# Attention and routed adapters on one core: PSUM planned by the bank, and new rules and priorities for the order of loads and work

## Chip, cores and metric

The kernel runs on one core of a Trainium2 chip. The metric is the device time of one execution in microseconds (us). Before the change three timed runs gave 164.81, 165.91 and 168.38 us; the median is 165.91.

## The reference

Inputs q, k and v have the shape (8 batches, 8 heads, 576 positions, 64). First comes attention in a sliding window, then a mixture of small adapters on its output:

```python
def _attn_ref(q, k, v):
    scores = scale * np.matmul(q, k.transpose(0, 1, 3, 2))      # scale = 1/sqrt(64)
    mask = np.abs(pos[:, None] - pos[None, :]) <= 32
    attn = softmax(np.where(mask, scores, -1e9))
    return np.matmul(attn, v)

def _moe_ref(x, w_gate, A, B):                                  # x: (4608, 512)
    logits = x @ w_gate                                         # 8 experts
    # the two largest logits of each row, softmax over the two: w
    # delta = sum over the two experts e of w_e * (x @ A[e]) @ B[e],  rank 16
    return x + delta
```

## The kernel before, in words

**Attention.** q and k arrive in nine tiles of 128 rows. A row is 16 consecutive positions of a head, for two heads (`raw`, three buffers for q and three for k). The loads are issued by GpSimd (`load`, L272, issue at L279) and turn float32 into float16 on the way. TensorE transposes a tile with 64 matmuls (`trans`, L360). VectorE copies q's transposes to `qT` (L367), ScalarE copies k's to `kT` (L372). A score task (`score`, L404 for the mask and L416 for the products) fills one 128x1024 float32 piece of PSUM, and ScalarE turns it into `PT` by an exp (L424). There are 36 score tasks. v comes in float32 by four loads per batch from the SP queue (`load_v`, L289) into two `vraw` buffers; GpSimd casts each half of a batch into one of three `vbd` buffers (`cast_v`, L339). A pv task (L465) multiplies PT by v for one pair of heads; there are four in a batch, 32 in all. VectorE divides by the row sums (`norm`, L483 and L484) and writes float16 rows `xs`.

**Adapters.** For each batch TensorE transposes `xs` (L518), VectorE copies the result to `xT` (L523), and TensorE makes the products with A and the gate weights (`moe_zl`, L531). ScalarE copies these to `zl` (L542), except for the last batch. The choice of two experts is a chain: two VectorE operations (L554, L555), an exp on ScalarE (L558), six on VectorE (L562 to L568), and two multiplications (`gate3`, L574 and L575), which run on GpSimd, on VectorE for the last batch. TensorE transposes the result `zs` (L581), ScalarE copies it to `zT` (L586), and TensorE makes delta plus x in pairs of matmuls (L594 and L596). ScalarE copies the sums to `ob` (L603) and SP stores them (L609, L614).

**What sets the order.** No order is written by hand. `Planner` (L24) runs once on the host when the kernel is built. Each piece of work is a task with an engine, an assumed duration, a due time, dependencies, and slots that it takes from and gives back to named pools. The planner steps through its own clock and starts, on each engine, the ready task with the lowest due time whose slots are free; DMA transfers are tasks on two modelled queues, Q0 for GpSimd's loads and Q1 for SP's. The start times that come out fix the order in which the instructions of each engine are issued (L654 to L660), and which buffer each task gets. On the chip each engine works in that order and waits on semaphores; the planner's times play no part there.

PSUM is four tiles `W0` to `W3` of 128x1024 float32, two banks each (L204). Every task that writes PSUM takes a whole `W`. A k load of tile t is made to follow, in the plan and so on GpSimd's queue, the first v cast of batch t-2, by `GATE` (L183), which is empty for tile 1. The adapter weights' loads follow the first load of the second v batch (`WDEP`, L185). Tile 0 is loaded and transposed in two halves (`SPLIT`).

Of the kernel before, what the change touches and what calls it, by code (L numbers as in the profile page):

```python
# [23 lines left out]
class Planner:  # L24
# [4 lines left out]
    STICK = 0.3  # L29
    SWITCH = 0.12  # L30
# [8 lines left out]

    def add(self, name, eng, dur, due, emit, deps=(), take=(), drop=(), lat=None, pkt=1.0,  # L40
            cap=1.0, mode=None):
        t = dict(name=name, eng=eng, dur=dur, due=due, emit=emit, deps=list(deps),
                 take=list(take), drop=list(drop), lat=self.LAT if lat is None else lat,
                 n=len(self.tasks), pkt=pkt, cap=cap, mode=mode)
        assert name not in self.by_name, name
        self.tasks.append(t)
        self.by_name[name] = t
        return name

    def run(self):  # L50
# [9 lines left out]
        held = {}  # L60
# [26 lines left out]
        while events:  # L87
# [17 lines left out]
            while drops and drops[0][0] <= now + 1e-9:  # L105
                _, _, (p, key) = heapq.heappop(drops)
                self.slots[p].append(held.pop((p, key)))
            for e in engines:
                if free_at[e] > now + 1e-9:
                    continue  # L110
                last_mode = mode.get(e)
                for t in sorted(ready[e], key=lambda t: (
                        t["due"] + (self.STICK if t["mode"] != last_mode else 0.0), t["n"])):
                    if all(self.slots[p] for p, _ in t["take"]):
                        break
                else:
                    continue
                ready[e].remove(t)
                for p, key in t["take"]:
                    s = self.slots[p].pop(0)  # L120
                    held[p, key] = s
                t["start"] = now
                end = now + t["dur"] + (self.SWITCH if t["mode"] != last_mode else 0.0)
                mode[e] = t["mode"]
                free_at[e] = end
                heapq.heappush(events, end)
                t["held"] = dict(held)
                done.append(t)
                finish(t, end)
# [16 lines left out]
def kernel(  # L146
# [36 lines left out]
    GATE = {t: [f"cv{t - 2}.0"] for t in range(2, 9)}  # L183
    GATE[1] = []
    WDEP = ["lv1.0.0"]  # L185
# [19 lines left out]
    W16 = [w.bitcast(F16) for w in W]  # L205

# [10 lines left out]
    P.pool("W", NW)  # L217
# [8 lines left out]
    P.pool("rc", 3)  # L226
    place = {}

    def slot(p, key):
        return place[p, key]  # L230

# [89 lines left out]
    for b in range(B):  # L321
        for n, (m0, m1) in enumerate(vparts(b)):
            for h in range(2):
# [3 lines left out]
                      prev, take=[] if n or h else [("vr", b)], lat=1.2)  # L327
                prev = [f"lv{b}.{n}.{h}"]
                P.add(f"dv{b}.{n}.{h}", VQ[h][2], 2.15 * (m1 - m0) / 36, 0, None, prev, lat=0.8,
                      pkt=14.7, cap=0.82)  # L330
    P.add("ldw", "SP", 2.0, -2, load_w, WDEP, lat=1.2)
    P.add("dw", "Q1", 1.7, -10, None, ["ldw"], lat=0.8, pkt=18.0)
# [20 lines left out]
    def trans(t, w, h0, h1):  # L353
        src = raw[2 * slot("raw" + "qk"[w], t) + w]
        tp = W16[slot("W", ("t", t, w, h0))].rearrange("p (h r i) -> p h r i", h=2, i=64)
        for r in range(RR):
            for h in range(h0, h1):
                p = slice(64 * h, 64 * h + 64)
                for hh in range(2):
                    nc.tensor.matmul(out=tp[64 * hh:64 * hh + 64, h, r],  # L360
# [3 lines left out]
    def evac(t, w, h0, h1):  # L364
        tp = W16[slot("W", ("t", t, w, h0))].rearrange("p (h r i) -> p h r i", h=2, i=64)[:, h0:h1]
        if w == 0:
            nc.vector.tensor_copy(  # L367
                out=qT[:, :, PADQ + 128 * t + 64 * h0:PADQ + 128 * t + 64 * h1].rearrange(
                    "p r (h i) -> p h r i", i=64),
                in_=tp)  # L370
        else:
            nc.scalar.copy(  # L372
                out=kT[slot("kT", t)][:, 64 * h0:64 * h1].rearrange("p (h i) r -> p h i r", i=64),
                in_=tp.rearrange("p h r i -> p h i r"))

    for t in range(NTI):
        hs = ((0, 1), (1, 2)) if t in SPLIT else ((0, 2),)
        for w in range(2):
            for y, (h0, h1) in enumerate(hs):
# [7 lines left out]
                      take=[("W", ("t", t, w, h0))] + ([("kT", t)] if w and y == 0 else []),  # L387
                      drop=[("raw" + "qk"[w], t)] if last else [])
                P.add(f"e{'qk'[w]}{t}.{y}", "ACT" if w else "DVE",
                      (0.2 + 1.5 * f) if w else (0.12 + 1.1 * f), due,  # L390
                      lambda t=t, w=w, h0=h0, h1=h1: evac(t, w, h0, h1),
                      [f"tr{t}.{w}.{y}"], drop=[("W", ("t", t, w, h0))])
# [6 lines left out]
    def score(t):  # L399
        ps = W[slot("W", ("s", t))].rearrange("p (e i c) -> p e i c", e=2, c=128)  # L400
# [22 lines left out]
    def expo(t):  # L423
        nc.scalar.activation(out=PTs[slot("PT", t)].rearrange("p e i c -> p (e i c)"),  # L424
                             in_=W[slot("W", ("s", t))],
# [12 lines left out]
    for t in range(NT):  # L438
        need = set()
        for g in blocks(t):  # L440
            lo, hi = 4 * g - 2, 4 * g + 5
            for z in (max(lo, 0), min(hi, NI - 1)):
                tt = z // 128
                need.add((tt, (z % 128) // 64 if tt in SPLIT else 0))
# [8 lines left out]
    def pv(u):  # L453
        b, n = divmod(u, NP)
        e, m = divmod(n, 2)
        po = W[slot("W", ("p", u))].rearrange("p (h c) -> p h c", h=2)
# [21 lines left out]
    def norm(u):  # L478
        b, n = divmod(u, NP)
        po = W[slot("W", ("p", u))].rearrange("p (h c) -> p h c", h=2)[:, :, 0:NG * VD]  # L480
# [29 lines left out]
    GX = ((0, 1, 2, 3), (4,))  # L510

    def moe_xT(b, j):
        x = xs[slot("xs", b)]
        tp = W16[slot("W", ("x", b, j))]
        for m, g in enumerate(GX[j]):
# [5 lines left out]
    def moe_ex(b, j):  # L521
        n = len(GX[j])
        nc.vector.tensor_copy(  # L523
            out=xT[b % 2][:, GX[j][0]:GX[j][0] + n].rearrange("p g c k -> p (g c k)"),
            in_=W16[slot("W", ("x", b, j))][:, 0:512 * n])

    def moe_zl(b):
        pz = W[slot("W", ("z", b))]
# [11 lines left out]
    def copy_z(b):  # L540
        pz = W[slot("W", ("z", b))][:, 0:GS * NG].rearrange("p (g c) -> p g c", c=GS)
        nc.scalar.copy(out=zls[b % 2], in_=pz[:, :, 0:ER + E])  # L542

    def zlog(b):
        if b in DIRECT:
            pz = W[slot("W", ("z", b))][:, 0:GS * NG].rearrange("p (g c) -> p g c", c=GS)
# [23 lines left out]
    def gate3(b):  # L570
        z = zlog(b)[0]
        lm, m2, s, gate = (gt[x][b % 2] for x in ("lm", "m2", "s", "gate"))
        eng = nc.vector if b in DIRECT else nc.gpsimd
# [3 lines left out]
    def moe_zT(b):  # L577
        zs = zss[b % 2].rearrange("p g e r -> p g (e r)")
        tp = W16[slot("W", ("y", b))]
# [4 lines left out]
    def moe_ez(b):  # L584
        tp = W16[slot("W", ("y", b))][:, 0:128 * NG]
# [3 lines left out]

    def moe_pd(b, j):  # L590
        pd = W[slot("W", ("d", b, j))].rearrange("p (i c) -> p i c", c=DD)
# [8 lines left out]
    def moe_eo(b, j):  # L600
        n = len(GG[j])
        pd = W[slot("W", ("d", b, j))].rearrange("p (i c) -> p i c", c=DD)
# [13 lines left out]
    for b in range(B):  # L616
        d0 = 4 * b + 4.6
        for j in range(2):
            n = len(GX[j])
            P.add(f"xT{b}.{j}", "PE", 0.24 * n, d0 + 0.1 * j, lambda b=b, j=j: moe_xT(b, j),  # L620
                  [f"nm{u}" for u in range(4 * b, 4 * b + 4)]
                  + ([f"zl{b - 2}"] if b >= 2 else []), take=[("W", ("x", b, j))], mode="full")
            P.add(f"exx{b}.{j}", "DVE", 0.1 + 0.28 * n, d0 + 0.1 * j - 0.5, lambda b=b, j=j: moe_ex(b, j),
                  [f"xT{b}.{j}"], drop=[("W", ("x", b, j))])
        P.add(f"zl{b}", "PE", 1.29, d0 + 0.5, lambda b=b: moe_zl(b),
              [f"exx{b}.{j}" for j in range(2)] + ["cw"], take=[("W", ("z", b))], mode="full")
        dr = b in DIRECT
        if not dr:
            P.add(f"cz{b}", "ACT", 0.85, d0 - 1, lambda b=b: copy_z(b), [f"zl{b}"]
# [4 lines left out]
        P.add(f"g2{b}", "DVE", 1.15, d0 - 1, lambda b=b: gate2(b), [f"ge{b}"])  # L634
        P.add(f"g3{b}", "DVE" if dr else "POOL", 1.05 if dr else 1.6, d0 - 1,
              lambda b=b: gate3(b), [f"g2{b}"], drop=[("W", ("z", b))] if dr else [])
        P.add(f"zT{b}", "PE", 0.32, d0 + 0.8, lambda b=b: moe_zT(b), [f"g3{b}"],
              take=[("W", ("y", b))], mode="full")
        P.add(f"ez{b}", "ACT", 0.7, d0 + 0.5, lambda b=b: moe_ez(b),
              [f"zT{b}"] + ([f"pd{b - 2}.2"] if b >= 2 else []), drop=[("W", ("y", b))])  # L640
        for j in range(3):
            n = len(GG[j])
            P.add(f"pd{b}.{j}", "PE", 0.44 * n, d0 + 1.2 + 0.7 * j, lambda b=b, j=j: moe_pd(b, j),
                  [f"ez{b}", "perm"] + ([f"pd{b}.{j - 1}"] if j else []),
                  take=[("W", ("d", b, j)), ("ob", (b, j))], drop=[("xs", b)] if j == 2 else [], mode="full")
            P.add(f"eo{b}.{j}", "ACT", 0.2 + 0.42 * n, d0 + 1.2 + 0.7 * j,
                  lambda b=b, j=j: moe_eo(b, j), [f"pd{b}.{j}"],
                  drop=[("W", ("d", b, j))])
            P.add(f"st{b}.{j}", "SP", 0.65 * n, d0, lambda b=b, j=j: moe_st(b, j),
# [44 lines left out]
```

## Time and profile before

| | |
|---|---|
| median of three timed runs | 165.91 us |
| device time of the profiled execution | 168.72 us |
| its span, first to last instruction | 167.0 us |
| mean granted TensorE clock | 0.877 |
| TensorE matmul busy | 104.2 us (62%), 3464 matmuls |
| ScalarE busy | 83.6 us (50%) |
| VectorE busy | 67.8 us (41%) |
| GpSimd busy | 54.0 us (32%) |
| DMA queue of SP (v, weights, stores) | 43824 packets, 19.42 MB, 44.2% of 16 engines |
| DMA queue of GpSimd (q, k) | 5152 packets, 9.44 MB, 33.3% |
| instruction queue q8 | 27 packets, 0.44 MB |

Engine names in the profile: PE is TensorE (PEld its weight loads), DVE VectorE, ACT ScalarE, POOL GpSimd, SP SyncE. A group of instructions is given by line, engine, operation, output and inputs, with the idle time just before it and what ended it ("<-"). "issue" is time in which an engine waited for nothing that the profile shows. In the slices, each digit is the busy share of a fortieth of the span in tenths, PEclk the granted TensorE clock in the same way.

### The profile page before, as it was taken

The numbers are of one execution on the slowest core, as the hardware profiler recorded it, in microseconds if no ns is written. First come the engines' busy times: TensorE is split into PE (matmuls) and PEld (weight loads), VectorE is DVE, ScalarE is ACT, GpSimd is POOL, SyncE is SP. The second block draws the span as 40 slices with busy tenths as digits, with TensorE's granted clock in tenths as the row PEclk, the third lists the DMA queues.
The fourth block names the chain that finished last, engine by engine and source line by source line (L and its number), as shares of the span: only waits on it lengthen the run. The fifth ranks groups of instructions, "written<-read, shape, count | busy, mean of one in ns | idle before, by whom it ended". The sixth has DMA issues, their size and how long they took to land.

```text
span 167.0 us, 7557 instructions
## 1 busy us (share of the span) xinstructions
PE 104.2 (62%) x3464; PEld 77.2 (46%) x3464; DVE 67.8 (41%) x164; ACT 83.6 (50%) x94; POOL 54.0 (32%) x76
## 2 busy tenths in 40 slices
PE   0259536480975857736478678775667989386350
PEld 0247425470864634326457554544457467274110
DVE  0011520270745625225265834763460958542300
ACT  3214706432044497584036479744669796416160
POOL 7950710745030779800000683900063030210000
PEclk9999955558589999996789999999999999959785
DMA  5999999999979669999996279999630254404434
GB/s 86 215 222 224 189 215 226 212 203 206 214 180 205 116 122 183 215 253 221 342 231 164 50 103 253 296 183 216 225 98 4 92 205 145 142 4 147 138 112 171
DMA packets 49008, 29.34 MB, mean 176 GB/s; under 512 B 39632, under 2 KB 39632, under 8 KB 48976
## 3 DMA queue, kind: packets, MB, share of 16 engines
q1 hardware_dynamic: 43824, 19.42, 44.2%
q0 software_dynamic: 5152, 9.44, 33.3%
q8 instruction: 27, 0.44, 1.1%
q14 instruction: 5, 0.04, 0.1%
HBM read 28.85 MB, written 9.44 MB: 229 GB/s over the span
## 4 chain that ended last, share of the span: by engine, by line
PE 39%; issue 30%; DMA 12%; DVE 6%; ACT 4%; POOL 4%; POOLq 1%; ACTq 1%; SPq 0%; DVEq 0%
PE W L518 6%; PE W L465 5%; PE W L360 5%; DMA vraw<-in_v_dram 5%; PE W L594 5%; DMA raw<-in_q_dram 5%; PE W L416 5%; PE W L596 4%; PE W L531 4%; PE W L404 4%; POOL vbd L339 2%; DMA out_dram<-ob 2%; DVE xs L484 2%; ACT PT L424 2%; DVE qT L367 1%
## 5 line engine op out<-in xcount | busy, mean ns | idle before, releaser
L424 ACT ACTIVATE PT<-W 128x1024 f16<-128x1024 f32 x36 | 35.6, 1031 | 29.1 <-PE W L416 25.0
L360 PE MATMUL W<-ident,raw 64*64 64x64 f16 x1152 | 18.6, 210 | 21.4 <-issue 10.9
L465 PE MATMUL W<-vbd,PT 64*64 64x65 f16 x1152 | 19.0, 205 | 16.0 <-issue 11.5
L339 POOL TENSOR_SCALAR_AFFINE_SELECT vbd<-vraw 128x1152 f16<-128x1152 f32 x16 | 20.3, 1274 | 25.6 <-DMA vraw<-in_v_dram 25.5
L603 ACT COPY ob<-W 128x1024 f32<-128x1024 f32 (+1 forms) x24 | 20.6, 872 | 15.7 <-PE W L596 13.0
L360 PEld LDWEIGHTS <-raw 64*64 64x64 f16 x1152 | 16.3, 123 | 22.9 <-issue 12.8
L484 DVE TENSOR_TENSOR xs<-W,rc 128x640 f16<-128x640 f32 x32 | 26.4, 825 | 1.1
L372 ACT COPY kT<-W 128x2048 f16<-128x2048 f16 (+1 forms) x10 | 17.0, 1698 | 18.7 <-PE W L360 18.7
L465 PEld LDWEIGHTS <-PT 64*64 64x64 f16 x1152 | 15.4, 118 | 21.0 <-issue 17.2
L483 DVE RECIPROCAL rc<-W 128x10 f32<-128x10 f32 x32 | 6.9, 217 | 42.2 <-PE W L465 41.3
L416 PE MATMUL W<-qT,kT 64*64 64x128 f16 x576 | 20.4, 246 | 4.3 <-issue 2.8
L574 POOL TENSOR_TENSOR gate<-lm,s 128x40 f32<-128x40 f32 x7 | 1.8, 253 | 65.0 <-DVE s L568 65.0
L416 PEld LDWEIGHTS <-kT 64*64 64x64 f16 x576 | 17.0, 124 | 10.1 <-issue 7.3
L367 DVE COPY qT<-W 128x2048 f16<-128x2048 f16 (+1 forms) x10 | 11.2, 1116 | 24.0 <-PE W L360 24.0
L518 PE MATMUL W<-ident,xs 128*128 128x128 f16 x160 | 14.2, 253 | 6.5 <-issue 5.5
L404 PE MATMUL W<-mask,ident 64*64 64x512 f16 x144 | 17.9, 458 | 0.0
L523 DVE COPY xT<-W 128x2048 f16<-128x2048 f16 (+1 forms) x16 | 12.5, 816 | 10.9 <-PE W L518 10.9
L594 PE MATMUL W<-Bsb,zT 128*128 128x512 f16 x40 | 16.4, 409 | 0.8 <-ACT zT L586 0.8
L518 PEld LDWEIGHTS <-xs 128*128 128x128 f16 x160 | 12.3, 126 | 8.4 <-issue 6.0
L596 PE MATMUL W<-xs,po__107 128*128 128x512 f16 x40 | 16.0, 401 | 0.0
L531 PE MATMUL W<-WA,xT 128*128 128x136 f16 x160 | 11.4, 226 | 1.7 <-issue 1.2
L531 PEld LDWEIGHTS <-xT 128*128 128x128 f16 x160 | 10.0, 99 | 3.0 <-issue 1.3
(40 smaller groups left out, 82.3 us busy)
## 6 DMA issues: line engine op xcount, KB each, us to landing
vraw<-in_v_dram SPq DMA_DIRECT2D x32, 288.0 KB, 7.3
out_dram<-ob SPq DMA_DIRECT2D x8, 512.0 KB, 9.9
out_dram<-ob SPq DMA_DIRECT2D x16, 192.0 KB, 3.6
out_dram<-ob SPq DMA_DIRECT2D x8, 256.0 KB, 2.9
raw<-in_k_dram POOLq DMA_DIRECT2D x4, 256.0 KB, 6.8
raw<-in_q_dram POOLq DMA_DIRECT2D x4, 256.0 KB, 6.1
raw<-in_k_dram POOLq DMA_DIRECT2D x2, 448.0 KB, 6.5
raw<-in_q_dram POOLq DMA_DIRECT2D x2, 448.0 KB, 7.7
```

The lines of the kernel that those rows point to most:

```text
L339: nc.gpsimd.affine_select(out=o, in_=i_, compare_op=ALU.is_ge, fill=0.0, base=1, channel_multiplier=0, pattern=[[0, m1 - m0], [0, D]])
L360: nc.tensor.matmul(out=tp[64 * hh:64 * hh + 64, h, r], lhsT=src[p, hh, D * r:D * r + D], rhs=ident[p, p], is_transpose=True, start=True, s ...
L404: nc.tensor.matmul(out=ps[o0:o0 + 64, e], lhsT=ident[p0:p0 + 64, p0:p0 + 64], rhs=bcast(mask[p0:p0 + 64].rearrange("p h r s -> p (h r s)") ...
L416: nc.tensor.matmul(out=ps[o0:o0 + 64, e, i], lhsT=kT[slot("kT", g // 32)][p0:p0 + 64, c1:c1 + 4].rearrange("p s r -> p (s r)"), rhs=qT[p0: ...
L424: nc.scalar.activation(out=PTs[slot("PT", t)].rearrange("p e i c -> p (e i c)"), in_=W[slot("W", ("s", t))], func=AF.Exp, scale=1.0 / floa ...
L465: nc.tensor.matmul(out=po[o0:o0 + 64, hh, c0:c0 + VD], lhsT=PTs[slot("PT", s // 4)][p0:p0 + 64, e, s % 4, 64 * (1 - j):64 * (1 - j) + 64], ...
L484: nc.vector.tensor_tensor(out=xs[slot("xs", b)].rearrange("p g (h m d) -> p h g m d", h=2, d=D)[:, :, :, n], in0=pog[:, :, :, 0:D], in1=bc ...
L518: nc.tensor.matmul(out=tp[:, o:o + 128], lhsT=x[:, g].rearrange("p (k c) -> p c k", c=4)[:, c], rhs=ident, is_transpose=True, start=True, ...
L531: nc.tensor.matmul(out=pz[:, GS * g:GS * g + ER + E], lhsT=xT[b % 2][:, g, c, :], rhs=WA_sb[:, c, :], start=(c == 0), stop=(c == NP - 1))
L594: nc.tensor.matmul(out=pd[:, i], lhsT=zTs[b % 2][:, g], rhs=B_sb, start=True, stop=False)
L596: nc.tensor.matmul(out=pd[:, i], lhsT=po_, rhs=x[:, g], start=False, stop=True)
L603: nc.scalar.copy(out=obs[slot("ob", (b, j))][:, 0:n], in_=pd[:, 0:n])
```

## The change

Six things change; the arithmetic and the number of matmuls do not.

1. The planner hands out PSUM by the bank: a pool `H` of eight banks, from which a task may take one bank ("H") or an aligned pair ("W"). A transposed tile takes two separate banks. Its two evacuations (qT, kT) become two copies of 128x1024 each, one per bank. The transposes of `xs` come in three pieces of up to two groups instead of two pieces of up to four; `zs` transposes and the third delta piece take one bank.
2. A pool `ring` of three slots is added in the plan: at most three v or weight transfers are outstanding there at once. Modelled durations of v transfers change, and a cap on Q1's rate goes.
3. `GATE`: tile 1's k load follows the first v cast of batch 0; tiles 3 to 8 keep theirs, tile 2 loses its own.
4. `WDEP`: the weights' loads follow the last load of the second v batch.
5. `gate3` runs on VectorE for all batches.
6. A table `LEAN` is added to the due times by kind of task, and several assumed durations change.

```diff
+    LEAN = {"cv": 4.05, "cvb": 0.12, "cz": 1.77, "ek": 0.68, "eo": 4.52, "eq": 0.17,
+            "ex": 1.69, "exx": -1.73, "ez": 0.2, "g2": -1.13, "g3": -0.98, "ge": -2.56,
+            "ld": 8.62, "ldw": 0.53, "lv": -0.54, "nm": -3.01, "pad": 0.06, "pd": 1.33,
+            "pv": -5.83, "sc": 0.22, "st": 3.31, "tr": -0.25, "xT": 3.08, "zT": 0.92,
+            "zl": -4.88}
...
+    def grab(self, p):
+        free = self.slots["H"]
+        if p == "W":
+            for s in free:
+                if s % 2 == 0 and s + 1 in free:
+                    free.remove(s)
+                    free.remove(s + 1)
+                    return s
+            return None
+        if p == "H":
+            best = [s for s in free if s ^ 1 not in free] or free
+            if not best:
+                return None
+            s = best[0]
+            free.remove(s)
+            return s
+        return self.slots[p].pop(0) if self.slots[p] else None
...
-        t = dict(name=name, eng=eng, dur=dur, due=due, emit=emit, deps=list(deps),
+        t = dict(name=name, eng=eng, dur=dur, due=due + self.LEAN.get(kind, 0.0), emit=emit, deps=list(deps),
...
-    GATE = {t: [f"cv{t - 2}.0"] for t in range(2, 9)}
-    GATE[1] = []
-    WDEP = ["lv1.0.0"]
+    GATE = {t: [f"cv{t - 2}.0"] for t in range(3, NTI)}
+    GATE[1] = ["cv0.0"]
+    WDEP = ["lv1.1.1"]
...
-    P.pool("W", NW)
+    P.pool("H", 2 * NW)
...
+    P.pool("ring", 3)
...
-                      prev, take=[] if n or h else [("vr", b)], lat=1.2)
+                      prev, take=[("ring", (b, n, h))] + ([] if n or h else [("vr", b)]), lat=1.2)
...
-                P.add(f"dv{b}.{n}.{h}", VQ[h][2], 2.15 * (m1 - m0) / 36, 0, None, prev, lat=0.8,
-                      pkt=14.7, cap=0.82)
+                P.add(f"dv{b}.{n}.{h}", VQ[h][2], 2.6 * (m1 - m0) / 36, 0, None, prev, lat=0.8,
+                      pkt=18.0, drop=[("ring", (b, n, h))])
...
-            nc.vector.tensor_copy(
-                out=qT[:, :, PADQ + 128 * t + 64 * h0:PADQ + 128 * t + 64 * h1].rearrange(
-                    "p r (h i) -> p h r i", i=64),
-                in_=tp)
+            c0 = PADQ + 128 * t + 64 * h
+            nc.vector.tensor_copy(out=qT[:, :, c0:c0 + 64], in_=tp)
         else:
-            nc.scalar.copy(
-                out=kT[slot("kT", t)][:, 64 * h0:64 * h1].rearrange("p (h i) r -> p h i r", i=64),
-                in_=tp.rearrange("p h r i -> p h i r"))
+            nc.scalar.copy(out=kT[slot("kT", t)][:, 64 * h:64 * h + 64],
+                           in_=tp.rearrange("p r i -> p i r"))
...
-                      take=[("W", ("t", t, w, h0))] + ([("kT", t)] if w and y == 0 else []),
+                      take=[("H", ("t", t, w, h)) for h in range(h0, h1)]
+                      + ([("kT", t)] if w and y == 0 else []),
...
     GG = ((0, 1), (2, 3), (4,))
-    GX = ((0, 1, 2, 3), (4,))
+    PB = {1: "H", 2: "W"}
...
-        eng = nc.vector if b in DIRECT else nc.gpsimd
+        eng = nc.vector
...
-        for j in range(2):
-            n = len(GX[j])
+        for j in range(3):
+            n = len(GG[j])
...
-        P.add(f"g3{b}", "DVE" if dr else "POOL", 1.05 if dr else 1.6, d0 - 1,
+        P.add(f"g3{b}", "DVE", 1.15, d0 - 1,
```

## The prediction

> **What bounds the kernel now.** I read the page's 40 slices first, then who waited for whom, then the timelines of TensorE and GpSimd with the idle time ahead of each group.
>
> ```profile
> PE   0259536480975857736478678775667989386350
> POOL 7950710745030779800000683900063030210000
> PEclk9999955558589999996789999999999999959785
> DMA  5999999999979669999996279999630254404434
> ```
>
> One slice is 4.2 us. DMA is full for some 50 us and again later, yet it pauses near 58, 92 and 125 us. GpSimd, which issues every q and k load, does nothing from 70 to 93 us. TensorE runs at half clock between 20 and 50 us.
>
> ```profile
> POOL gate L574 <- DVE s L568: 65.0, 7, 22.9
> ...
> PE W L465 <- issue: 11.5, 7, 4.0
> PE W L360 <- issue: 10.9, 6, 2.6
> ...
> PE W L360 <- DMA raw<-in_k_dram: 6.8, 2, 5.8
> ...
> PE W L360 <- DMA raw<-in_q_dram: 2.9, 3, 1.9
> ...
> PE W L465 <- DVE qT L367: 1.7, 1, 1.7
> ```
>
> GpSimd's 65 us is one queue standing behind seven gates. It looks like the find, but TensorE waits for DMA 9.7 us in all.
>
> ```profile
> 19.94 0.41 PE L360 MATMUL W<-ident,raw 64*64 64x64 f16 x26 [0.35 <-DMA raw<-in_q_dram]
> 23.00 0.74 PE L360 MATMUL W<-ident,raw 64*64 64x64 f16 x38 [2.65 <-issue]
> ...
> 119.88 0.49 PE L465 MATMUL W<-vbd,PT 64*64 64x65 f16 x36 [1.67 <-DVE qT L367]
> ...
> 128.70 0.23 PE L465 MATMUL W<-vbd,PT 64*64 64x65 f16 x5 [0.93 <-issue]
> ...
> 143.76 0.64 PE L465 MATMUL W<-vbd,PT 64*64 64x65 f16 x52 [1.04 <-ACT PT L424]
> 146.68 0.71 PE L581 MATMUL W<-ident,zs 128*128 128x128 f16 x5 [2.28 <-POOL zs L575]
> ```
>
> The last DMA wait of TensorE ends at 19.94 us. After it TensorE is the path: it is busy, or it has an "issue" gap, or it waits briefly for an evacuation. There are 20 issue gaps after 20 us, 32.0 us together. Between the gaps ending at 23.00 and starting at 27.75 lie 128 matmuls, each with its weight load: 256 instructions. The DMA table shows 27 instruction-queue packets, 0.44 MB. So a gap is a block of instructions arriving late: 0.93 us with DMA idle, up to 3.98 us with DMA full.
>
> ```profile
> 11.40 1.18 POOL L279 DMA_DIRECT2D raw<-in_q_dram  x2
> 17.80 1.26 POOL L339 TENSOR_SCALAR_AFFINE_SELECT vbd<-vraw 128x1152 f16<-128x1152 f32 x1 [5.22 <-DMA vraw<-in_v_dram]
> ...
> 93.18 0.25 POOL L574 TENSOR_TENSOR gate<-lm,s 128x40 f32<-128x40 f32 x1 [22.91 <-DVE s L568]
> ```
>
> **What the skill says.** The Trainium skill, "Runtime: NRT & Kernel Launch", Instruction fetch mechanics: instructions stream in 16 KiB blocks of 256 and the cost is mostly hidden. The block size agrees with the trace (0.44 MB in 27 packets, 128 matmuls between gaps); "hidden" does not, 32 us show. "TensorE: Matmul & The Clock Gate", Part 1: the clock is halved after an idle window of about 3.4 us and restored by a busy one. The trace agrees in kind: half clock after the gaps at 20 to 50 us, and 147.2 to 149.3 us after the 2.28 us wait. "DMA: Bandwidth & Descriptors", Queues, rings and completion order: the engines take turns between queues. Here q and k (software queue) and v (hardware queue) share full engines from 3 to 50 us.
>
> **The change part by part**, against the profiled span of 167.0 us (device time of that execution 168.72; the median of the three timed runs is 165.91, and I take the difference off the median).
>
> *Start.* As built, the k load of tile 1 now follows the first cast of v batch 0 (10.16 us) and its q load follows the second cast. That cast began at 17.80 after a DMA wait and held GpSimd to 19.02, so q issues at about 19.0 instead of 11.40, with v ahead perhaps 1 us sooner because k starts later. The part of 448 KB is issued second, about 18.6 to 19.5. It took 7.9 us to land in the trace, part of that queued behind k; alone in its queue I estimate 4.5 to 7.9, and take 24 us. Tile 1's q transposes then end at 24.7 instead of 23.74. The late fetch of 2.65 us hides in that wait, because the matmul that waits is 26 matmuls ahead of the block edge. Evacuating by halves (0.69 us, the 128x1024 row, instead of 1.22) gives 0.5 back at the scores. Behind q stand, on GpSimd, the four issues of tile 2 (2.3 us), about 1 us later than at 19.02; tile 2's q transposes had a 2.51 us fetch gap of their own that absorbs it. I charge +1.0; ends -0.5 (v sooner) and +4 (late landing and fetch in series). The four v loads of batch 1 now go ahead of the weights on SP, 3 x 2.2 us of issue (5 issues took 11.21 us). The weights' cast ran at 35.4 and is first needed at 46 us; in the new vector order it follows all eight norms of batches 0 and 1, and the routing matmul follows that: 0.
>
> *Gates.* Seven gates leave GpSimd (7 x (0.25+1.28) = 10.7 us, and the 65 us of standing) and go to VectorE at 0.20+0.83 = 1.03 us each, +7.2 us. Freed q/k loads run earlier into the pauses, but no load is waited for after 20 us: 0. SP's order of v against stores shifts too: the sixth v batch stands behind stores of batch 2 (near 98 us), first needed near 125; the seventh behind stores of batch 3 (near 114), needed near 136. With 8 us to land and 1.3 us of cast both fit: 0, but only some 10 us of cover.
>
> *PSUM by bank.* Copies of 2048 become two of 1024: 8 for qT and 8 for xT at 2x0.69-1.22 = 0.16, +2.6 us VectorE; 8 for kT at 2x1.01-1.87 = 0.15, +1.2 us ScalarE. VectorE goes to 67.8+7.2+2.6 = 77.6 us of 167, hidden if the order lets it. What it buys are TensorE's evacuation waits from 25 to 144 us: 0.59, 0.46, 0.27, 0.85, 0.23, 0.43, 0.48, 1.67, 0.27, 0.27, 1.04 = 6.56 us. By the new instruction order I strike out 1.67 (the pv's now precede tile 7's transposes), 1.04 (both last exps precede batch 5's output copies on ScalarE), 0.85 and 0.48 (waits for a whole two-bank slot), 0.46 (another batch's routing matmuls stand ahead): 4.5. For new waits I put back 1.0, a choice. Net -3.5; ends -6.6 and +6.
>
> *Priorities, tail.* The order of TensorE is close to the old one until the end. Before, the last pv ends at T = 144.4 and the span 22.6 us later. Now batch 6's transposes (1.35), routing (1.18) and the last delta of batch 5 (0.43) come after the last pv: T is 2.95 us earlier. The new tail from T: delta 0.45; transposes of 6 and 7 to 3.15; their six VectorE copies to 4.4; routing to 5.55; gates of both, one VectorE chain of 0.4+1.0+1.0 us per batch, with ScalarE's exps, from 5.1 to 9.9; transposes, copy of zT to 10.5; first two delta pairs at half clock (0.43 a matmul, as at 158 us) to 12.2; then six output copies on ScalarE, 0.92 or 0.5 each with slips, to 17.8; the last 0.9 MB of stores at the 340 GB/s seen from 153 us take 2.6, and the end about 2 more: 22.9. So +0.3; ends -2 and +6.
>
> Sum: +1.0 -3.5 -2.95 +0.3 = -5.1, or 161.9 in the span and 160.8 in the median's terms.
>
> **Rivals.** *Loads did matter* (fuller DMA earlier, fewer fetches meeting full queues). The pauses at 56 to 64 us (share 0.62, 3.0 us free) and 88 to 100 (0.52, 5.8) would be filled; half of 8.8 gives 156.4. For it: gaps shrink to 0.93 when DMA is idle. Against: the bytes are the same, so full time only moves. *Waits replaced*: the banks give nothing net, the -3.5 goes, 164.3. For it: waits of an in-order engine move to the next late thing. *VectorE becomes the bound* (other side): gates and halved copies sit in the one queue that also frees every pv's banks; all of it exposed is +9.8, 170.6. It decides once norms queue behind gate chains more than the one pv that other banks can take. For it: VectorE was busy 3.65 of 4 us at 92 to 96, and each chain holds the queue while ScalarE's exp comes. Against: its norms waited 41.3 us for TensorE. *Slow tail*: half clock through the whole tail costs 4x0.8 for four blocks of 20 and 2.8 more on the deltas, 166.8.
>
> **Chances.** Forecast 0.40 (own range 158 to 163.5; 0.33 of it faster by over 2%, 0.07 within), loads 0.15, replaced waits 0.18, VectorE 0.19, slow tail 0.08 (0.06 within, 0.02 slower). Faster than 162.6: 0.48; within: 0.31; slower than 169.2: 0.21; 2% is about what this measurement tells from nothing. The range 155 to 171 reaches from the loads case to the VectorE case with the ends of start and tail.
>
> **What would show it.** Right: no gate rows on GpSimd and its 65 us gone; tile 1's q wait growing from 0.35 to some 4 us with the following issue gap gone; about 20 issue gaps of 30 us still there; TensorE's evacuation waits from 25 us to the last pv near 3; the last pv near 139; a tail of 23 us with two gate chains in it. Wrong: new DMA waits of TensorE after 30 us, norms late behind gates, issue gaps summing under 25 or over 38, or half clock after the last pv.

## The result and the profile after

The changed kernel takes 173.75 us (median of four runs, 172.66 to 175.43) against 166.32 for the kernel before beside it. The ratio is 1.046, with a 95% interval of 1.032 to 1.059: slower, where I had forecast 160.8. Here and below, ratios and their intervals compare the quicker runs of each kernel (those within 1.5% of its fastest), while medians and ranges in brackets behind a time take in all its runs. The profiled execution after took 172.66 us, span 171.0, and is one of its quicker ones; the one of before took 168.72, span 167.0, and is one of its slower ones. So the two profiles differ by 4.0 us where the medians differ by 7.4.

The slices after, 4.3 us each:

```profile
PE 109.6 (64%) x3464; PEld 81.3 (48%) x3464; DVE 76.1 (45%) x194; ACT 83.6 (49%) x102; POOL 43.3 (25%) x62
...
PE   0249555478259459947764299782596989863940
...
POOL 7657800154554360020505000502022000000000
PEclk9999999999858957999999558997559999996597
DMA  4999999999999978897894504999970053520284
```

TensorE is busy 5.4 us longer than before (104.2), with the same 3464 matmuls. The clock shows where. The first clock records lie at 16.8 us in the profile before and at 38.8 us in that after, and the page counts the time ahead of them as full clock, which it was not: the 38 transposes at 23.84 us after (shown in the part on why the prediction was wrong) take 0.74 us, as long as those at 23.00 us before, which lie in recorded half clock. So the page's means of 0.877 and 0.873 can't be compared. From 40 us on both profiles have records. There, half clock stands before at 41 to 48, 75 to 78 and 82 to 85 us, and after at 46 to 53, 59 to 66, 93 to 104 and 117 to 128 us, until the last pv. The next table cuts from 40 us to the end of the last pv, and from there to the end. The columns are the window, its length, the busy time of PE, PEld, DVE, ACT and POOL, then the granted clock, DMA share and GB/s; first the kernel before, then the changed one:

```profile
40.00:144.40 104.40, 74.52 (x2661) 55.41 (x2660) 52.42 (x124) 61.40 (x71) 32.40 (x39) 0.93 0.79 182
144.40:167.00 22.60, 10.56 (x70) 6.30 (x70) 6.32 (x20) 6.55 (x9) 1.53 (x2) 0.77 0.31 106
```

```profile
40.00:146.40 106.40, 75.81 (x2627) 55.84 (x2626) 57.96 (x145) 60.87 (x76) 23.61 (x28) 0.84 0.76 170
146.40:171.00 24.60, 12.94 (x112) 8.19 (x110) 8.54 (x28) 8.68 (x13) 0.00 (x0) 0.81 0.41 142
```

A clock of 0.84 over 106.4 us is 34 us at half clock, against 14 before. The middle is longer, and TensorE busier in it by 1.3 us, although 42 more matmuls now stand in the tail; its idle time there is nearly the same (30.6 and 29.9 us).

Who waited for whom, after:

```profile
POOL vbd L385 <- DMA vraw<-in_v_dram: 77.2, 14, 16.3
...
PE W L407 <- issue: 12.4, 7, 2.9
PE W L563 <- issue: 7.7, 2, 4.6
...
PE W L510 <- issue: 6.7, 3, 3.4
PE W L407 <- ACT kT L417: 6.2, 5, 2.1
```

The 65 us behind gates are gone from GpSimd; it now stands behind casts that wait for v. The issue gaps add up to 28.1 us in 14 gaps (32.0 in 20 before). New is the fourth PE line: transposes of q take banks that the copy of k is only just leaving.

The largest gap and what follows it, on TensorE, and how the loads of tile 8 came to lie there, on SyncE and then GpSimd:

```profile
121.45 1.87 PE L563 MATMUL W<-ident,xs 128*128 128x128 f16 x16 [4.58 <-issue]
...
125.94 2.13 PE L576 MATMUL W<-WA,xT 128*128 128x136 f16 x20
```

```profile
81.25 2.75 SPq L335 DMA_DIRECT2D vraw<-in_v_dram  x3
103.94 0.80 SPq L664 DMA_DIRECT2D out_dram<-ob  x2
104.79 0.60 SPq L335 DMA_DIRECT2D vraw<-in_v_dram  x1
```

```profile
108.81 1.26 POOL L385 TENSOR_SCALAR_AFFINE_SELECT vbd<-vraw 128x1152 f16<-128x1152 f32 x1 [16.28 <-DMA vraw<-in_v_dram]
110.02 0.73 POOL L325 DMA_DIRECT2D raw<-in_k_dram  x1
110.75 0.73 POOL L325 DMA_DIRECT2D raw<-in_q_dram  x1
```

SyncE stands 20 us behind the first store of batch 2. The second v load of batch 6 is queued behind it, the cast behind that load, and tile 8's q and k behind the cast. They then share the DMA engines with v loads and stores when TensorE's next instruction block is due. Late they were before, too: there tile 8's loads were issued at 105.5 and 107.6 us, some 3 to 4.5 us earlier, and the same block edge showed a gap of 1.67 us (119.88 us in the prediction, put down to the copy of q).

### The profile page after: what moved, and what is told of

Same layout as the page of the kernel before. It is cut to its first block, busy times and chain, and to the rows that moved or that the text cites. A ratio compares the mean times of both kernels' runs of the same rounds, so it can differ in the third digit from the quotient of the medians.

```text
span 171.0 us, 7576 instructions
## 1 busy us (share of the span) xinstructions
PE 109.6 (64%) x3464; PEld 81.3 (48%) x3464; DVE 76.1 (45%) x194; ACT 83.6 (49%) x102; POOL 43.3 (25%) x62
## 4 chain that ended last, share of the span: by engine, by line
PE 48%; issue 20%; ACT 14%; DVE 9%; DMA 4%; POOL 1%; ACTq 0%; DVEq 0%; POOLq 0%
PE W L407 9%; PE W L563 8%; PE W L576 5%; PE W L644 5%; PE W L510 5%; PE W L461 5%; PE W L646 5%; ACT PT L469 4%; PE W L449 4%; DMA raw<-in_k_dram 4%; ACT kT L417 4%; ACT ob L653 3%; DVE xs L529 2%; PE W L626 2%; DVE xT L568 2%
## 5 line engine op out<-in xcount | busy, mean ns | idle before, releaser
L407 PE MATMUL W<-ident,raw 64*64 64x64 f16 x1152 | 20.6, 218 | 29.1 <-issue 12.4
L407 PEld LDWEIGHTS <-raw 64*64 64x64 f16 x1152 | 18.2, 130 | 31.6 <-issue 22.1
L417 ACT COPY kT<-W 128x1024 f16<-128x1024 f16 x18 | 17.8, 1029 | 18.7 <-PE W L407 18.7
L510 PE MATMUL W<-vbd,PT 64*64 64x65 f16 x1152 | 17.9, 203 | 9.6 <-issue 6.7
L415 DVE COPY qT<-W 128x1024 f16<-128x1024 f16 x18 | 11.8, 685 | 25.9 <-PE W L407 20.5
L528 DVE RECIPROCAL rc<-W 128x10 f32<-128x10 f32 x32 | 6.9, 216 | 29.4 <-PE W L510 27.6
L568 DVE COPY xT<-W 128x1024 f16<-128x1024 f16 (+1 forms) x24 | 13.5, 595 | 14.1 <-PE W L563 13.3
L461 PE MATMUL W<-qT,kT 64*64 64x128 f16 x576 | 18.8, 241 | 1.3 <-issue 0.8
L449 PE MATMUL W<-mask,ident 64*64 64x512 f16 x144 | 17.8, 452 | 0.7 <-issue 0.5
L646 PE MATMUL W<-xs,po__107 128*128 128x512 f16 x40 | 17.3, 433 | 0.0
L587 ACT COPY zl<-W 128x680 f32<-128x680 f32 x7 | 5.1, 727 | 21.8 <-PE W L576 21.8
L576 PEld LDWEIGHTS <-xT 128*128 128x128 f16 x160 | 11.6, 110 | 0.1
```

The costliest lines, as they stand in the source:

```text
L407: nc.tensor.matmul(out=tp[h][64 * hh:64 * hh + 64, r], lhsT=src[p, hh, D * r:D * r + D], rhs=ident[p, p], is_transpose=True, start=True, s ...
L417: nc.scalar.copy(out=kT[slot("kT", t)][:, 64 * h:64 * h + 64], in_=tp.rearrange("p r i -> p i r"))
L449: nc.tensor.matmul(out=ps[o0:o0 + 64, e], lhsT=ident[p0:p0 + 64, p0:p0 + 64], rhs=bcast(mask[p0:p0 + 64].rearrange("p h r s -> p (h r s)") ...
L461: nc.tensor.matmul(out=ps[o0:o0 + 64, e, i], lhsT=kT[slot("kT", g // 32)][p0:p0 + 64, c1:c1 + 4].rearrange("p s r -> p (s r)"), rhs=qT[p0: ...
L510: nc.tensor.matmul(out=po[o0:o0 + 64, hh, c0:c0 + VD], lhsT=PTs[slot("PT", s // 4)][p0:p0 + 64, e, s % 4, 64 * (1 - j):64 * (1 - j) + 64], ...
L576: nc.tensor.matmul(out=pz[:, GS * g:GS * g + ER + E], lhsT=xT[b % 2][:, g, c, :], rhs=WA_sb[:, c, :], start=(c == 0), stop=(c == NP - 1))
```

## The experiments

A few terms: *block gap* is an issue gap at the edge of 256 TensorE instructions. Runs named together ran on one chip; beside them the kernel before took 167.15 (first four), 166.2 (next four), 166.04 (the s runs), 165.73 (the t runs) and 166.49 (the u runs).

**1. Undo one part at a time.** Each of these but the gate run is planned anew, so its whole order moves.

```
r1   LEAN = {}
r2   GATE, WDEP, v durations as before; pool "ring" out
r3   eng = nc.vector if b in DIRECT else nc.gpsimd        # place in the program kept
r4   if p in "WH": take an aligned pair                    # every task a whole two-bank tile
```

> The changed kernel with every planner priority of the new table at zero; all other parts of the change stay. Theory A (instruction blocks arrive late behind q and k data while the load order bunches them, each late block is followed by half clock): the loads of the last two tiles are then issued at other times, so the three gaps of 3.1, 3.4 and 4.6 us near 92, 98 and 121 us should move or shrink, but the sum of the issue gaps stays at 25 to 32 us; 169 to 175. Theory C (the priorities are the cause, by the order of the last two batches): the tail from the last pv shrinks from 24.7 us to 22 or less and the time returns to 166 to 168. Theories B (gates on VectorE), D (load waits and queue order), E (PSUM by the bank): no change, 172 to 175.

> The changed kernel with the loads ordered as before: the same load waits, the weights after the first load of batch 1, no ring of three for the v loads, and the old planner costs of v; gates, banks and priorities stay as changed. Theory D (the new load waits and order are the cause): 166 to 168, the large gaps after 90 us gone, since q and k of the last two tiles are issued before 75 us again. Theory A: the same direction, 166 to 170, if the issue times do move; if they stay bunched it stays at 172 to 175. B, C, E: 172 to 175.

> The changed kernel with the last two gate operations of batches 0 to 6 on GpSimd, each at the place in the program at which VectorE did them; nothing else moves. Theory B (the gates on VectorE are the cause): VectorE is freed of 7 us, and the time falls to 166 to 169. A, C, D, E: the gates were hidden on VectorE; the time stays at 172 to 175, or gets longer by 1 to 3 us, as GpSimd stands behind gates again and issues loads and casts later.

> The changed kernel with PSUM handed out by whole two-bank tiles as before; the copies keep their halves, and loads, gates and priorities stay as changed. Theory E (banks reused at once make the transposes of q wait for the copy of k): the 6.2 us of waits of the transposes for the copy of k fall to under 2 and the time to 166 to 169. A, B, C, D: waits for whole tiles come back instead, 172 to 176. My forecast had priced the banks at a gain of 3.5 us: if that part is right, the time goes up to 176 or more.

Measured: without the priorities 176.11 (ratio 1.063, 1.047 to 1.078); with the old load order 174.72 (171.2 to 175.8); with the gates back on GpSimd 175.08 (1.057, 1.041 to 1.073); with whole tiles 167.12 (1.010, 0.996 to 1.024). Only undoing the banks brings the time back, to within -0.4 and +2.4% of that before. Undone alone, neither the gates on VectorE (theory B) nor the priorities (C) nor the load order (D) gives the 7 us back. What the expectation for the old load order says of the kernel before is mistaken: q and k of its last two tiles were issued at 96 to 107.6 us, not before 75.

**2. Banks or order?** The order is frozen and only the bank of each task is chosen anew, by a table that takes the one freed longest ago.

```
+ place.update({(p, k): BANK[p, k] for p, k in t["held"] if p in "HW"})
```

> The changed kernel with every instruction in the order it has now; only which PSUM bank each task gets is chosen anew, by a fixed table, so that a task takes the bank that was freed the longest time ago. Undoing the banks in the run before brought the time back to that of the kernel before, but it moved the whole order too. Theory E1 (the reuse of a just freed bank is the cause): the transposes' waits for the copy of k fall from 6.2 us to under 2, the evacuation waits of TensorE between 25 us and the last pv from 8.7 to under 4, and the time to 167 to 169. Theory A (late instruction blocks and half clock in this order of the work): the waits fall, but the three large gaps after 90 us stay; 170 to 174.

> The kernel of the whole two-bank tiles (167.1 us) with its own order of instructions kept, and only the banks chosen anew by a fixed table, one bank where one is enough, the one freed the longest ago. Theory E1 (which bank is taken decides): 1 to 4 us faster than 167.1, that is 163 to 166. Theory A (the order against instruction blocks and loads decides): within 1.5 us of 167.1.

In the changed order the wait for k's copy fell as meant,

```profile
PE W L407 <- ACT kT L417: 1.3, 1, 1.3
```

from 6.2, but all of TensorE's evacuation waits from 25 us to the last pv fell only from 8.7 to 7.5, not under 4: most of these waits stayed with the order. The time stayed at 174.29 (170.07 to 174.47). In r4's order the table gave 169.49 (1.022, 1.013 to 1.031), no gain on r4's 1.010. So it is not the choice of a just-freed bank, which I could read straight off the profile. What is left is the order that the planner finds for banks, with the waits that belong to it.

**3. No v traffic.**

```
+ if b >= 2: return        # in load_v
```

> The changed kernel without the v loads of batches 2 to 7: their casts read the v of batches 0 and 1 again, so the output is not the reference's; all else stays in its order. Half of the DMA time is gone. Theory A: blocks of instructions then meet at most q and k data; gaps fall from 28 us to under 18, and the time to 155 to 162, to within 3 us of the kernel before treated alike. Theory E1 (bank waits): only what the gaps give both kernels goes; the difference of 6 to 7 us to the kernel before stays.

> The kernel before without the v loads of batches 2 to 7, as in the run beside it (output not the reference's). Theory A: 153 to 160, gaps after 20 us under 20 instead of 32. Theory E1: 6 to 7 us under the changed kernel treated alike. If neither kernel gets 4 us faster, data on the DMA engines is not what makes blocks late.

Changed kernel 164.99 (162.3 to 165.4), kernel before 159.23 (ratio 0.960, 0.952 to 0.969). Both gain 7 to 9 us: data on the DMA engines does cost. Between the two, 5.8 us are left by the medians, but only 3.9 by the lowest runs (162.27 and 158.42). So this pair does not decide between theory A, within 3 us, and a difference that stays.

**4. The queue chain of tile 8.** Order of TensorE, VectorE and ScalarE frozen; the plan's list is rearranged for one queue.

```
s1   behind("lv6.0.1 lv6.1.0 lv6.1.1 lv7.0.0 lv7.0.1 lv7.1.0 lv7.1.1 st2.0", "cv5.1")
s2   behind("ld7.0.0 ld8.1.0 ld8.0.0", "ld7.1.0")
```

> The changed kernel again, unaltered, on the chip of the runs beside it. All theories: 172.5 to 175.5, a ratio to the kernel before of 1.03 to 1.06. It shows how far one profiled execution differs from the next: the order of the work is the same, so the large gaps near 92, 98 and 121 us should come back within 2 us of their places if they belong to the order of the loads, and move if they are chance.

> The changed kernel with only SyncE's queue put in another order: the last three v loads of batch 6 and the four of batch 7 go ahead of the first store of batch 2. In the changed kernel that store holds SyncE from 84.0 to 103.9 us, the first cast of batch 6 waits for the v load behind it until 108.8, and the q and k loads of tile 8 stand behind that cast until 110.0. Theory F (this queue chain bunches loads against late instruction blocks): tile 8 is issued near 93 to 100, the gap of 4.6 us near 121 and the half clock after it go, and the time falls to 168 to 170.5. Theory G (the order in which TensorE takes up the work is slow by itself, wherever the loads land): 172.5 to 175.5, the lost time shows at other blocks.

> The changed kernel with only GpSimd's queue put in another order: the q load of tile 7 and both loads of tile 8 are issued at once behind the k load of tile 7, near 83.5 to 86 us, ahead of three v casts, instead of at 91.4 and 110.0. Theory F: no q and k traffic is left after 96 us; the gaps near 98 and 121 us shrink from 3.4 and 4.6 to under 1.5 each with no half clock after them, 167.5 to 170.5. Theory G: 172.5 to 175.5.

> The changed kernel with both queues reordered as in the two runs beside it. Theory F: 166 to 170, the DMA engines idle from about 105 us but for stores. Theory G: 172.5 to 175.5. If the v loads brought forward fill the engines from 84 to 98 us and the blocks there are late instead, the gain of each alone is lost again.

Unaltered 174.5 (171.0 to 179.3); v first 172.57 (169.5 to 177.6); q and k early 171.81 (1.032, 1.020 to 1.044); both 171.68 (1.028, 1.016 to 1.041). The place of the gap is no chance: at the block edge after matmul 2652 it is 4.58 and 4.15 us in the two profiles of the unaltered kernel, 1.69, 1.56 and 1.96 in the three others, where tile 8 was issued at 95.5, 87.2 and 87.4 us instead of 110.0 and 114.1. In s2 that edge reads

```profile
120.09 1.32 PE L563 MATMUL W<-ident,xs 128*128 128x128 f16 x16 [1.56 <-issue]
```

The gap near 98 us, however, stayed in s2 (3.41 us at 100.4): the loads brought forward were in front of that block instead, where q and k took 69% of the DMA engines' time from 95 us to the end of the gap. Full engines alone did not make the gap at the edge large: in s2 they were full ahead of its 1.56 us as well, with v and stores alone. Theory F is right about the mechanism at this edge. It is worth some 2 us of the 7, and the intervals do not even make sure of those 2. Half clock from 40 us to the last pv did not fall with the time (34 and 31 us unaltered, 31 to 38 in the three others).

**5. No late q and k traffic: the quiet pair.**

```
+ if t >= 3: return        # in load
```

> The changed kernel without the q and k loads of tiles 3 to 8: the transposes read the data of the first three tiles again, so the output is not the reference's; all else stays in its order. Theory F (q and k data in front of instruction blocks make the difference): 158 to 163, within 2 us of the kernel before treated alike, no issue gap over 2.5 us after 60 us. Theory G (the order of the work is slow by itself): it stays 5 to 8 us above the kernel before treated alike.

> The kernel before without the q and k loads of tiles 3 to 8, as in the run beside it (output not the reference's). Theory F: 158 to 162, since it has fewer large gaps with these loads in front. Theory G: 155 to 159, with the changed kernel 5 to 8 us above.

Changed kernel 161.02 (160.9 to 161.8; ratio 0.981, 0.972 to 0.990), kernel before 152.88 (0.926, 0.911 to 0.942). Each gains some 13 us, the kernel before landing below both ranges, and the difference is 8.1 us, not less. Theory F as the whole cause has fallen: the order is slower without these data too. But the runs of the changed kernel now lie within 0.9 us, so the two halves of part 2 could be asked again:

> The changed kernel in its own order, without the q and k loads of tiles 3 to 8 (output not the reference's), and with the banks chosen by the fixed table of the earlier run, the one freed longest ago. Beside 161.0 for the same without the table. Theory E1 (waits of the transposes for a bank just freed, 4 to 6 us, and the half clock that they bring): 153 to 157. Theory G (the order): 159.5 to 162.

> The kernel whose PSUM is handed out by whole two-bank tiles (all other parts of the change as they are, planned anew; 167.1 with all loads), without the q and k loads of tiles 3 to 8 (output not the reference's). Beside 161.0 for banks and 152.9 for the kernel before. Theory G (the order that the planner finds for banks is the slow one): 152 to 156. If it stays at 159 to 162, the order with whole tiles is no better by itself, and its 167.1 came from where its loads meet the blocks.

Banks by the table in the changed order: 161.35 (161.1 to 162.1). The order planned for whole tiles: 156.24 (154.9 to 157.3), just above the range given. So with less DMA traffic too, it is the order planned for banks and not the choice of a bank. The table took the waits for k's copy from 4.7 to 1.7 us in these profiles, but the issue gaps rose from 13.2 to 18.5. Whole tiles give back 4.8 of the 8.1 us; the rest, 3.4 us between 156.24 and 152.88, stays with the other parts of the change. In these four profiles, from 40 us to the last pv, in the order t2 (kernel before), u2 (whole tiles), t1 (changed), u1 (changed, table):

```profile
40.00:128.60 88.60, 72.58 (x2648) 52.90 (x2645) 52.86 (x125) 60.81 (x72) 21.40 (x22) 0.96 0.53 143
```

```profile
40.00:129.90 89.90, 71.37 (x2629) 53.11 (x2627) 58.72 (x145) 60.29 (x76) 12.58 (x10) 0.92 0.47 126
```

```profile
40.00:134.80 94.80, 74.47 (x2581) 54.34 (x2572) 58.47 (x143) 59.99 (x75) 12.95 (x11) 0.87 0.45 123
```

```profile
40.00:136.10 96.10, 74.93 (x2637) 56.00 (x2630) 59.31 (x145) 60.77 (x76) 12.71 (x10) 0.88 0.44 119
```

The clock goes with the time: 0.96, 0.92, 0.87, 0.88 beside medians of 152.9, 156.2, 161.0, 161.4. Over the whole span TensorE is busy 102.9 us in t2 and 107.9 in t1: the matmuls are the same, so 5.0 of the 8.2 us of span go with slower ones, and the other 3.2 are idle time. Two places show how half clock comes about. The first is the block edge of the 4.58 us gap. In t1's order it lies behind the transposes of tile 7, k then q, in those of a batch's `xs`; the timeline and two windows:

```profile
105.62 0.69 PE L409 MATMUL W<-ident,raw 64*64 64x64 f16 x62 [0.71 <-ACT ob L655]
106.25 0.47 PE L565 MATMUL W<-ident,xs 128*128 128x128 f16 x5
108.50 1.02 PE L565 MATMUL W<-ident,xs 128*128 128x128 f16 x15 [1.79 <-issue]
...
110.66 1.86 PE L565 MATMUL W<-ident,xs 128*128 128x128 f16 x16
```

```profile
105.90:109.40 3.50, 1.71 (x73) 1.51 (x57) 0.77 (x2) 1.93 (x2) 0.00 (x0) 0.99 0.98 252
109.40:112.80 3.40, 3.26 (x43) 2.83 (x42) 2.38 (x5) 1.02 (x1) 1.27 (x1) 0.50 0.89 204
```

TensorE is busy 1.71 of 3.5 us, and the next window is halved: 16 transposes of the full array take 1.86 us, where 15 took 1.02 before it. The wait of 0.71 us lies ahead of the clock's own window here (105.95 to 109.36 us), so the one late block of 1.79 us was enough. But this place does not set the orders apart. The kernel before has the same gap at the same edge, in a window with the same busy share of 0.48, and kept its full clock:

```profile
105.61 0.48 PE L467 MATMUL W<-vbd,PT 64*64 64x65 f16 x35 [1.78 <-issue]
```

The second place has no late block, and no data moves. In t1's order the q transposes of the last tile stand close behind those of k, with one pv between them, which waits for an exp; q's then wait for k's copy to leave a bank, and ScalarE makes the exp and the copy one after the other:

```profile
117.42 0.48 PE L512 MATMUL W<-vbd,PT 64*64 64x65 f16 x36 [1.13 <-ACT PT L471]
117.83 0.22 PE L409 MATMUL W<-ident,raw 64*64 64x64 f16 x2
119.23 0.83 PE L409 MATMUL W<-ident,raw 64*64 64x64 f16 x62 [1.18 <-ACT kT L419]
```

```profile
116.20:119.60 3.40, 1.09 (x85) 0.88 (x87) 2.98 (x11) 3.38 (x5) 0.00 (x0) 1.00 0.00 0
119.60:123.00 3.40, 3.40 (x74) 3.13 (x62) 1.42 (x3) 1.20 (x2) 0.00 (x0) 0.50 0.03 5
```

With the table (u1) 0.41 and 1.33 us of these two waits are left, and the next window is halved too. In the kernel before (t2) the last tile's two sets of transposes stand 3.4 us apart with other work between them, and no window from 107 us to the last pv but the one that the tail cuts into is under 0.86 busy. It is one place, though: with all loads the same two waits are 0.42 and 1.18 us, and the clock stays full.

**6. One part alone on the kernel before.**

```
t3   eng = nc.vector                       # gates only, order kept
t4   after, with LEAN, GATE, WDEP, ring, v durations and gates as before; a few assumed durations stay as changed
```

> The kernel before with one part of the change alone: the last two gate operations of batches 0 to 6 on VectorE, each at the place in the program that it has on GpSimd; nothing else moves. My forecast priced this part at 0: 164 to 168. Theory F: GpSimd no longer stands behind gates for 65 us, so q and k of tiles 7 and 8 are issued near 82 and 92 us instead of 96 and 106; the blocks then meet other data, 163 to 169. Theory B (gates in the queue of VectorE delay the norms): 168 or more.

> The changed kernel with loads, gates and priorities as before, so that only PSUM by the bank and the copies by halves are left of the change, all planned anew. Forecast of my step: 162 to 163. Theory E2 (banks let the planner put work in an order that is slower on the chip): 170 to 176, with the loads of tile 8 issued after 105 us and a gap of over 3 us behind them. Theory H (only banks together with the new priorities are slow): 164 to 168.

Gates alone: 168.07 over 21 runs that spread from 162.2 to 178.6, eight of them above the highest of the 23 runs of the kernel before (162.8 to 168.9). The ratio is 0.993 (0.981 to 1.004). So no gain is shown, and a loss in many runs is not excluded. The profile, of a run at 175.22 us, has 37 us of half clock between 40 us and the last pv, where the kernel before had 14, and 3.4 us less idle time there: the same order of TensorE's work can run at either clock. Banks alone: 170.54 (1.030, 1.010 to 1.049), tile 8 issued at 108.0 and a gap of 4.84 us at 122.1. With r4, which keeps the halved copies and those durations and is not shown to be slow, this puts it on the banks, as E2 had it. The priorities, which come on top, are not excused: r1 without them is no faster.

## Why the prediction was wrong

*What bounds it.* Right: TensorE is the path. The first sign that I set out as showing me wrong, waits for DMA after 30 us, did not come; in the profile after all of TensorE's DMA waits (6.9 and 1.7 us) end before 11 us.

*Start, +1.0.* Measured +0.8 (tile 1's q transposes end at 24.59, before 23.75). The size held by luck, the working did not: q was issued at 15.30, not 19.0, the wait was for k's copy and not for q's data, and the issue gap behind it was still there:

```profile
21.99 0.58 PE L407 MATMUL W<-ident,raw 64*64 64x64 f16 x26 [2.06 <-ACT kT L417]
23.84 0.74 PE L407 MATMUL W<-ident,raw 64*64 64x64 f16 x38 [1.27 <-issue]
```

In the second profile of the same kernel (s0) the forecast's sign did come: a wait of 5.27 us for q's data, to 25.65, with no issue gap behind it. So one profile does not fix this term.

*Gates, 0.* Not settled. In the changed kernel no difference by the gates is shown (r3); alone on the kernel before they left a wide spread (t3). VectorE's busy time rose to 76.1 (I had 77.6), and its norms still wait for TensorE (27.6 us), so VectorE did not become the bound in this profile.

*SP's order, 0.* I saw that batch 6's v loads would stand behind a store of batch 2 and asked only when the data are needed. What I did not follow is the rest of the queue: behind that load a cast, behind the cast tile 8's loads, and their traffic in front of a block. The price is of the order of 2 us (part 4).

*Banks, -3.5: the step that failed.* TensorE's evacuation waits from 25 us to the last pv came to 8.7 us, not 3 (before 6.6): the new order brought waits of its own, where I had put back 1.0 by choice. And I had priced an order by striking out single waits at the old durations and keeping the stretch between them, when with new stalls the same matmuls run at another clock. The sum had no term for that: half clock stood only in the tail. Between 40 us and the last pv it went from 14 to 34 us. An estimate of what that cost: TensorE is busy 1.3 us longer there, though by my own figures 2.95 us of work left it, together 4.2 us. So the last pv, which came 7.4 us later than forecast, has 5.6 us of waits against it and 4.2 of slower matmuls, less 2.4 us of issue gaps that went (29.3 to 26.9 us from 25 us on). That lowering the waits would have helped is not shown either: the table took off 1.2 us in f1 and 2.9 in u1 (11.4 to 8.5), and the time did not change.

*Tail.* T came at 146.35, not 139: the 2.95 us of work did leave, and the stretch before it grew by more. The tail took 24.6, not 22.9. The gates of both batches were done about when I said (10.2 us from the last pv, 9.9 forecast). Then came nine matmuls of the deltas at half clock where I had four, 0.43 us each instead of 0.22, so the last output copy ended at 19.1 us and not at 17.8:

```profile
149.89 2.53 PE L576 MATMUL W<-WA,xT 128*128 128x136 f16 x40
155.66 0.71 PE L626 MATMUL W<-ident,zs 128*128 128x128 f16 x5 [3.24 <-DVE zs L620]
...
157.64 0.63 PE L644 MATMUL W<-Bsb,zT 128*128 128x512 f16 x1
158.07 0.63 PE L646 MATMUL W<-xs,po__107 128*128 128x512 f16 x1
...
161.81 0.38 PE L644 MATMUL W<-Bsb,zT 128*128 128x512 f16 x1
162.03 0.38 PE L646 MATMUL W<-xs,po__107 128*128 128x512 f16 x1
```

The routing ahead of it ran at full clock: 40 matmuls in 2.53 us, where at half clock 20 took 2.13 (at 125.94 above). The forecast's own parts of the tail add up to 22.4, not 22.9.

*Sum.* In the profiles: start +0.8, middle +1.1, tail +2.0, together +3.9 of the 4.0, where I had -5.1. "Waits replaced" had the right direction, "slow tail" the right mechanism, but most of it in another place, and the issue gaps (28.1, inside my 25 to 38) the wrong comfort: their sum may stay while their place changes the clock.

*What stays open.* No run changed the clock alone, so that half clock carries 5.0 of the 8.2 us is an account of busy time and not an experiment. No run took away v and the late q and k together, so where the remaining v loads meet TensorE's blocks in each order is not ruled out as a part of the difference. Why the orders that the planner finds for banks are slower on the chip than those for whole tiles is not settled; its clock knows neither blocks nor a second TensorE speed. With all loads the link is looser than in the quiet runs: f2 was profiled at 167.63 us with 34 us of half clock between 40 us and the last pv, as much as the changed kernel.

## What to carry to other kernels

When one engine is the path and its clock depends on how busy it has been, look at where the low clock lies and not at its mean (and at whether the clock was recorded there), and price a new order by stretches of work between stalls, not by adding and striking single waits. A transfer that nobody waits for can still cost, by what it stands in front of; follow a delayed queue to its last member. To find which part of a change costs, undo parts one at a time, and where the runs scatter take traffic away from both kernels until they do not.

## What the runs showed of the hardware

The clock records come in multiples of 3.41 us, on a fixed grid in each execution. The Trainium skill, "TensorE: Matmul & The Clock Gate", Part 1, says that the clock is halved after an idle window and gives the rule of no idle gap above some 3.4 us. The grid agrees with the traces; the condition is wider here. Over the 20 profiled executions, from each one's first clock record on, TensorE's busy share in each window against the clock of the next:

| window's clock | busy share | windows | next at half clock |
|---|---|---|---|
| full | under 0.4 | 93 | 93 |
| full | 0.4 to 0.5 | 32 | 26 |
| full | 0.5 to 0.6 | 45 | 14 |
| full | over 0.6 | 368 | 1 |
| half | under 0.7 | 106 | 106 |
| half | 0.7 to 0.8 | 28 | 24 |
| half | over 0.8 | 127 | 1 |

No window has to be idle: in t1 one stall of 1.79 us was enough, where in t2 one of 1.78 us was not. And no window at half clock that was under 0.7 busy was the last one at half clock; over 0.8 nearly all were.

The second thing is how much data cost an engine that does not wait for them: without q and k of six tiles out of nine the kernels gained 13 us each, though TensorE's waits for those loads after 30 us had been nil in the profiles of both.
